# Remainders of up to 32 tokens as a small call on raw weights, in a mixture-of-experts kernel

## The chip, the cores and the metric

One NeuronCore of a Trainium2 chip. The metric is the device time of one execution in microseconds. Engines: PE is TensorE, PEld its weight loads, DVE VectorE, ACT ScalarE, POOL GpSimd, SP the engine that issues most DMAs. "PEldq", "POOLq" and the like are the sequencers' own instructions (loads of registers, branches, waits), which are not counted as busy. [...]

## The reference

Block attention over 4 batches of 768 tokens gives x, 3072 rows of 512. A gate sends each token to one of 8 experts, one after another, and the expert's two layers make the output:

```python
for b in range(B):
    prev_e = -1
    for s in range(S):
        fresh_e = int(np.argmax(logits[b, s]))
        if s == 0 or local_gate[b, s] < 0.5:
            e = fresh_e
        else:
            e = prev_e if prev_e >= 0 else fresh_e
        prev_e = e
        ls = logits[b, s] - logits[b, s].max()
        p = np.exp(ls)
        p /= p.sum() + 1e-09
        h = np.maximum(x[b, s] @ w1[e], 0.0)      # 512 -> 1024
        out[b, s] = p[e] * (h @ w2[e])            # 1024 -> 512
```

Expert weights are 2 x 2 MB of fp32. How many tokens an expert gets depends on the data.

## The kernel before, in words

**Stages.** Attention runs to about 150 us; it writes x to DRAM. The expert calls begin at 133 us and run to the end. Tokens are sorted by expert into 42 slots of 128 rows; slots 0 to 5 (three pairs) are filled early, from the first batches, with the most frequent expert of batch 0 and a second one. `finish` (L782) places the rest: it counts blocks per expert, gives each a first slot, marks in `words` which slots start an expert and which expert comes next, and makes with `rows` (L870) and L961 to L975 the lists `gidx`, `sidx` and `psort` (which token rows a slot gathers, where its results go, and the gate's weight). Its steps are small DVE operations with a few PE products (L884, L949, L971) in between.

**A planner** (`later`, `small`, `flow`, L407 to L471) puts these steps between the matmuls of the running pairs: it keeps a modelled time for PE and for DVE (0.1 us for a small DVE step, 0.9 for a long one, 0.8 for PE) and writes each step where the model says that its input is ready. The order on each engine is then fixed.

**Calls.** `pair` (L1042) handles 256 tokens: for each of 8 column blocks of w1, 4 k-chunks x 3 products of fp32r halves (L1053 to L1055; weights and tokens are split into a high and a low part), then w2 for each half (L1026 to L1028), `store` (L1030: scaling by `psort`, then an indirect DMA to the output at L1039). `single` (L1078) does 128 tokens. Between the matmuls stand the next call's token transposes (`tx`, L1012) and the splitting of the next expert's weights (`split`, L982: ACT makes the high part, DVE or POOL the low one), under `tc.If(new > 0)` (L1234), then the refill of the staging buffer by DMA from SP.

**Order of the calls.** Slots 0 to 15 are eight fixed pairs. From slot 16 on, two slots at a time, a flag decides at run time whether it is a pair or a single; from slot 24 on, a test ends the loop:

```python
nb = reg(2 * SLOTS, mybir.ALL_ENGINES, SLOTS)
with ExitStack() as c:
    for i in range(2 * PAIRS, SLOTS, 2):
        if i >= NT:
            c.enter_context(tc.If(nb > i - EARLY))          # L1295
        two = reg(i + 1, mybir.ALL_ENGINES, 1)
        with tc.If(two > 0) as full:                        # L1298
            ... self.pair(i // 2, *calls(i + 2))
        with full.Else():
            self.single(i, *calls(i + 2))
```

`reg` (L1202) loads a word into a register of each engine named. In the code of every engine the single's instructions stand behind the pair's, and a body that is not run is jumped over; where a skipped body would have raised semaphores, the engine raises them itself, having waited for its own earlier work. A pair has some 310 PE instructions (matmuls and weight loads), a single some 140.

Of the kernel before, what the change touches and what calls it, by code (L numbers as in the profile page):

```python
# [34 lines left out]
PAIRS = 8  # L35
# [29 lines left out]
class Kernel:  # L65
    def __init__(self, ctx, tc, qT, kT, vT, vW, maskc, identc, wgc, w1, w2, c32c, cb16c, out):
# [49 lines left out]
        self.adj = cst.tile([P, 4, E], F32, name="adj")  # L116
        self.zero = cst.tile([P, P], F32, name="zero")
        self.words = cst.tile([1, 2 * SLOTS + 1], I32, name="words")
        self.gidx = cst.tile([P, SLOTS], I32, name="gidx")
        self.sidx = cst.tile([P, SLOTS], I32, name="sidx")  # L120
        self.psort = cst.tile([P, SLOTS], F32, name="psort")
# [3 lines left out]
        for t in (self.zero, self.cnt, self.carx, self.cum):  # L125
            tc.nc.gpsimd.memset(t, 0.0)
# [502 lines left out]
    def second(self):  # L629
# [28 lines left out]
        v.tensor_scalar(out=self.adj[:, 0], in0=self.er, scalar1=-2.0 * 4097, scalar2=6.0 * 4097 + 41344, op0=ALU.mult, op1=ALU.add)  # L658
        yield "DVE"
        v.tensor_scalar(out=self.adj[:, 1], in0=self.er, scalar1=-2.0 * P, scalar2=P - 1.0, op0=ALU.mult, op1=ALU.add)  # L660
        yield "DVE"
        v.tensor_scalar(out=self.adj[:, 3], in0=self.er, scalar1=-2.0 * P, scalar2=2.0 * P - 1.0, op0=ALU.mult, op1=ALU.add)
# [119 lines left out]
    def finish(self):  # L782

        nc, c, cum, wk = self.nc, self.c, self.cum, self.fw
# [9 lines left out]
        v.tensor_scalar(out=npi, in0=nbi, scalar1=8, scalar2=None, op0=ALU.logical_shift_right)  # L794
# [3 lines left out]
        v.tensor_tensor(out=nci, in0=self.cnt[:, B], in1=self.adj[:, 3], op=ALU.add)  # L798
        yield "DVE"
        v.tensor_scalar(out=nci, in0=nci, scalar1=8, scalar2=None, op0=ALU.logical_shift_right)  # L800
# [42 lines left out]
        for b in range(B):  # L843
            yield "DVE"
            v.tensor_tensor(out=t2[:, b], in0=self.oh[:, b], in1=pk.to_broadcast([P, E, NU]), op=ALU.mult)
        pt = wk.tile([P, NT, 1], I32, name="pt")
        yield "DVE"
        with nc.allow_low_precision(reason="whole numbers below 2**24"):
            v.tensor_reduce(out=pt[:, :, 0].rearrange("p (b u) -> p b u", b=B), in_=t2.rearrange("p b e u -> p b u e"),
                            op=ALU.add, axis=AX.X)  # L850
# [40 lines left out]
        start = wk.tile([P, 2, E], F32, name="start")  # L891
# [21 lines left out]
        lv = wk.tile([P, 2, E], F32, name="lv")  # L913
        yield "DVE"
        v.tensor_tensor(out=lv, in0=end, in1=start, op=ALU.is_ge)
# [6 lines left out]
        v.scalar_tensor_tensor(out=en, in0=start, scalar=lane, in1=en, op0=ALU.is_le, op1=ALU.mult)  # L922
        lve = wk.tile([P, 2, E], F32, name="lve")
        yield "DVE"
        v.tensor_tensor(out=lve, in0=lv, in1=c["iota"][:, 0:E].unsqueeze(1).to_broadcast([P, 2, E]), op=ALU.mult)
# [3 lines left out]
        wd = wk.tile([P, 2, 2, E], F32, name="wd")  # L929
# [3 lines left out]
        v.scalar_tensor_tensor(out=wd[:, 1], in0=start, scalar=cend, in1=lve, op0=ALU.is_equal, op1=ALU.mult)  # L933
# [14 lines left out]
        for i in range(2):  # L948
            nc.tensor.matmul(out=m[0:1, SLOTS * i:SLOTS * i + SLOTS], lhsT=w2[:, i:i + 1], rhs=self.ident[:, 0:SLOTS],  # L949
                             start=True, stop=True)  # L950
        yield "DVE"
        v.tensor_copy(out=self.words[:, 2 * SLOTS:], in_=tot)
        yield "DVE"
        v.tensor_copy(out=self.words[:, 0:2 * SLOTS], in_=m[0:1, 0:2 * SLOTS])
# [7 lines left out]
        v.tensor_tensor(out=eq, in0=c["iota"][:, EARLY:SLOTS].unsqueeze(1).to_broadcast([P, NT, n]),  # L962
# [11 lines left out]
        v.tensor_reduce(out=self.psort[:, EARLY:SLOTS], in_=m[:, 0:3 * n].rearrange("p (i s) -> p s i", i=3),  # L974
                        op=ALU.add, axis=AX.X)  # L975
        self.have_p = SLOTS


    def fetch(self, dst, which, c0, c1, e):
# [407 lines left out]
```

## Time and profile before

| | us |
|---|---|
| median of 3 runs | 469.2 (468.76 to 470.35) |
| profiled execution | 469.57, its span 467.8 |
| PE busy in the span | 433.9 (93%) |
| DVE, ACT, POOL busy | 254.4, 213.3, 226.2 |
| last matmul ends | 456.07 |

How to read it: busy times are shares of the span from the first to the last instruction. An engine's idle time is put down to the event that ended it. A group of instructions by line has its count, the total and the mean; a line of windows has the busy time of each engine in one stretch, with the number of instructions in brackets, then the granted clock (PEclk), DMA's busy share and GB/s.

### The profile page before, as it was taken

Reading aid. Unit: us, or ns where it says so; the run is one execution under the profiler, and the core shown is the slowest. Engines: PE = TensorE matmul, PEld = TensorE weight load, DVE = VectorE, ACT = ScalarE, POOL = GpSimd, SP = SyncE. Lnnn points to the kernel's source line nnn. Section 1 sums busy time; section 2 is a strip of 40 time slices with the busy share of each in tenths; the row PEclk is TensorE's granted clock in tenths of the full one; section 3 lists DMA queues with packets and bytes.
Section 4 is the critical chain, followed back from the end, with each engine's and each line's share of the span. In section 5 each row is a group of like instructions: output and inputs, shape, how many; then the busy total and the mean of one; then the engine's idle time right before and its main releaser. Section 6 shows DMA issues by size and latency. Waiting matters only on the chain. (4 is left out here: it accounts for less than half of the span.)

```text
span 467.8 us, 11959 instructions
## 1 busy us (share of the span) xinstructions
PE 433.9 (93%) x4360; PEld 379.9 (81%) x4360; DVE 254.4 (54%) x587; ACT 213.3 (46%) x464; POOL 226.2 (48%) x316
## 2 busy tenths in 40 slices
PE   7799989889699999999999999999999999999990
PEld 6587768767499798888989898988789898978970
DVE  4776797898855788971222222363563227265510
ACT  4888787887645126322212121454582127267300
POOL 2677675687405324912020202193976308488720
PEclk9989999999889999999999999999999999999996
DMA  8999979998230750742020202066579204848940
GB/s 303 378 378 375 378 253 406 377 342 315 89 138 2 262 232 25 275 160 85 12 80 10 82 12 82 6 211 240 205 294 361 85 24 133 320 140 301 320 152 27
DMA packets 23622, 92.04 MB, mean 197 GB/s; under 512 B 2927, under 2 KB 3567, under 8 KB 19440
## 3 DMA queue, kind: packets, MB, share of 16 engines
q1 hardware_dynamic: 18752, 76.11, 43.7%
q0 software_dynamic: 4640, 14.68, 9.9%
q8 instruction: 41, 0.67, 0.6%
q14 instruction: 45, 0.37, 0.2%
q10 hardware_dynamic: 144, 0.20, 0.1%
HBM read 78.40 MB, written 13.11 MB: 196 GB/s over the span
## 5 line engine op out<-in xcount | busy, mean ns | idle before, releaser
L1055 PE MATMUL bs<-xT,l 128*128 128x256 f32 x384 | 109.0, 284 | 1.0 <-DVE l L987 1.0
L1053 PE MATMUL bs<-xT,h 128*128 128x256 f32 x384 | 109.8, 286 | 0.0
L1054 PE MATMUL bs<-xT,h 128*128 128x256 f32 x384 | 108.8, 283 | 0.2 <-DVE xT L1004 0.2
L998 POOL DMA_INDIRECT xg<-x_dram,gidx x32 | 36.8, 1149 | 120.8 <-PE bt L1009 52.3
L1059 ACT ACTIVATE hT<-bs 128x512 fp32r<-128x512 f32 x48 | 28.7, 598 | 121.8 <-PE bs L1055 121.1
L1061 DVE SCALAR_TENSOR_TENSOR hT<-bs,hT 128x512 fp32r<-128x512 f32 x48 | 33.1, 690 | 85.6 <-ACT hT L1059 74.4
L1026 PE MATMUL ba<-h,hT 128*128 128x512 f32 x192 | 77.6, 404 | 0.4
L1028 PE MATMUL ba<-h,hT 128*128 128x512 f32 x192 | 75.0, 391 | 0.0
L1027 PE MATMUL ba<-l,hT 128*128 128x512 f32 x192 | 75.0, 391 | 0.0
L1055 PEld LDWEIGHTS bs<-xT,l 128*128 128x128 f32 x384 | 73.5, 191 | 1.9 <-DVE l L987 1.9
L1054 PEld LDWEIGHTS bs<-xT,h 128*128 128x128 f32 x384 | 73.5, 192 | 1.0 <-DVE xT L1004 0.4
L1053 PEld LDWEIGHTS bs<-xT,h 128*128 128x128 f32 x384 | 73.5, 191 | 0.9 <-issue 0.4
L992 POOL TENSOR_TENSOR l<-stg,h 128x256 fp32r<-128x256 f32 x84 | 73.1, 906 | 2.2 <-ACT h L984 1.6
L984 ACT CAST h<-stg 128x1024 fp32r<-128x1024 f32 x56 | 57.2, 1052 | 11.9 <-PE ba L1028 10.9
L282 ACT ACTIVATE pr<-bs,nm 128x120 f32<-128x120 f32 x192 | 51.9, 371 | 11.5 <-DVE nm L278 9.8
L987 DVE TENSOR_TENSOR l<-stg,h 128x1024 fp32r<-128x1024 f32 x35 | 46.7, 1342 | 16.2 <-ACT h L984 13.1
L1039 POOL DMA_INDIRECT out_dram<-yo,sidx x26 | 28.9, 1113 | 48.8 <-DVE yo L1038 21.3
L1026 PEld LDWEIGHTS ba<-h,hT 128*128 128x128 f32 x192 | 36.1, 188 | 8.1 <-issue 0.5
L1028 PEld LDWEIGHTS ba<-h,hT 128*128 128x128 f32 x192 | 36.0, 188 | 7.9
L1027 PEld LDWEIGHTS ba<-l,hT 128*128 128x128 f32 x192 | 36.2, 188 | 6.2
L243 POOL COPY vw<-vs 24x384 f32<-24x384 f32 x64 | 32.6, 550 | 8.6 <-ACT vs L238 6.1
L278 DVE TENSOR_REDUCE nm<-bs 128x6 f32<-128x720 f32 x32 | 28.8, 901 | 9.2 <-ACT vs L238 4.0
(236 smaller groups left out, 649.3 us busy)
## 6 DMA issues: line engine op xcount, KB each, us to landing
stg<-in_w SPq DMA_DIRECT2D x32, 1024.0 KB, 7.5
vw<-in_vW SPq DMA_DIRECT2D x16, 780.0 KB, 7.1
kp<-in_kT SPq DMA_DIRECT2D x16, 384.0 KB, 6.5
q<-in_qT SPq DMA_DIRECT2D x16, 384.0 KB, 7.5
vt<-in_vT SPq DMA_DIRECT2D x16, 384.0 KB, 8.2
x_dram<-xs SPq DMA_DIRECT2D x8, 768.0 KB, 3.9
wst<-in_w SPq DMA_DIRECT2D x8, 512.0 KB, 5.8
xg<-x_dram,gidx POOLq DMA_INDIRECT x32, 3.5
```

What stands on the lines that cost most here:

```text
L282: nc.scalar.activation(out=pr[:, h, u, :], in_=sp[:, h, u, :], func=AF.Exp, bias=nm[:, h, u:u + 1], scale=1.0)
L984: self.nc.scalar.copy(out=hi, in_=src)
L987: eng.tensor_tensor(out=lo, in0=src, in1=hi.bitcast(F32), op=ALU.subtract)
L992: eng.tensor_tensor(out=lo[:, p], in0=src[:, p], in1=hi[:, p].bitcast(F32), op=ALU.subtract)
L998: self.nc.gpsimd.indirect_dma_start(out=t, out_offset=None, in_=rows, in_offset=bass.IndirectOffsetOnAxis(ap=self.gidx[:, i:i + 1], axis=0))
L1026: nc.tensor.matmul(out=ps, lhsT=ah, rhs=wh, start=first, stop=False)
L1027: nc.tensor.matmul(out=ps, lhsT=ah, rhs=wl, start=False, stop=False)
L1028: nc.tensor.matmul(out=ps, lhsT=al, rhs=wh, start=False, stop=last)
L1053: nc.tensor.matmul(out=ps[:, j], lhsT=wh, rhs=xh, start=(k == 0), stop=False)
L1054: nc.tensor.matmul(out=ps[:, j], lhsT=wh, rhs=xl, start=False, stop=False)
L1055: nc.tensor.matmul(out=ps[:, j], lhsT=wl, rhs=xh, start=False, stop=(k == KT - 1))
L1061: nc.vector.scalar_tensor_tensor(out=l, in0=ps, scalar=0.0, in1=h.bitcast(F32), op0=ALU.max, op1=ALU.subtract)
```

## The change

An expert whose last block holds 1 to 32 tokens (the count plus 127, modulo 128, below 32) no longer gets that block as a slot. It goes to one of up to 8 further columns of the lists (slots 42 to 49), and is computed by `few`: 32 gathered rows, transposed; w1 as fetched, in fp32, without splitting; four column quarters of the product written to four groups of 32 PSUM partitions; then w2 in the same way, four groups of 128 output columns; one scaling and one indirect store of 128 rows of 128 columns. The weights have their own 32 KB per partition, where the lists' temporary tiles were (now in a pool of their own, closed before). The fixed pairs are 7 instead of 8, so the loop with run-time flags starts at slot 14, and its test at slot 22. Small call 0 stands behind the last fixed pair, calls 1 and 2 behind slots 16 and 20, any others behind the loop. Each has a flag and is jumped over if it isn't set; its weights and rows are fetched when the call before it is done.

```diff
-PAIRS = 8
+PAIRS = 7
+FEW = 32
+ALL = SLOTS + E
+CALLS = 11
+FEW_AT = (16, 20)
...
         v.tensor_tensor(out=nbi, in0=self.cnt[:, B], in1=self.adj[:, 1], op=ALU.add)
         yield "DVE"
-        v.tensor_scalar(out=npi, in0=nbi, scalar1=8, scalar2=None, op0=ALU.logical_shift_right)
+        v.tensor_scalar(out=npi, in0=nbi, scalar1=P - 1, scalar2=None, op0=ALU.bitwise_and)
+        lv = wk.tile([P, 3, E], F32, name="lv")
+        few = lv[:, 2]
+        yield "DVE"
+        v.tensor_scalar(out=few, in0=npi, scalar1=float(FEW), scalar2=None, op0=ALU.is_lt)
...
         self.have_words()
-        yield from rows(FIRST, SLOTS)
+
+        yield "DVE"
+        v.scalar_tensor_tensor(out=pk[:, :, 0], in0=self.er, scalar=2.0, in1=nbi, op0=ALU.mult, op1=ALU.add)
...
+        yield from by_expert()
...
+        v.copy_predicated(out=blk, mask=e1, data=pt)
+        yield from rows(FIRST, ALL)
         yield from self.gate_p(B - 1, B)
         yield from self.until(("weights", 0), ("weights", 2))
-        n = SLOTS - EARLY
+        n = ALL - EARLY
...
+        rs = wk.tile([P, 2, E], F32, name="rs")
+        yield "DVE"
+        v.tensor_copy(out=rs[:, 0], in_=self.sidx[:, SLOTS:])
+        yield "DVE"
+        v.tensor_copy(out=rs[:, 1], in_=self.psort[:, SLOTS:])
+        yield "PE"
+        m = self.bank("t")
+        for g in range(4):
+            nc.tensor.matmul(out=m[32 * g:32 * g + 32, 0:2 * E], lhsT=self.ident[:, 0:32], rhs=rs.rearrange("p i e -> p (i e)"),
+                             start=True, stop=True)
...
+    def few_in(self, j, e):
+        nc = self.nc
+        for w in range(2):
+            for c in range(0, KT * DF, 2048):
+                self.fetch(self.few_w[w][:, c:c + 2048], w, c, c + 2048, e)
+        nc.gpsimd.indirect_dma_start(out=self.few_x, out_offset=None, in_=self.x_rows,
+                                     in_offset=bass.IndirectOffsetOnAxis(ap=self.gidx[0:FEW, SLOTS + j:SLOTS + j + 1], axis=0))
+
+    def few(self, j):
+        nc, fw = self.nc, self.fw
+        w1, w2 = self.few_w
+        m = self.bank("t")
+        for k in range(KT):
+            nc.tensor.transpose(out=m[:, FEW * k:FEW * k + FEW], in_=self.few_x[:, P * k:P * k + P], identity=self.ident[0:FEW, 0:FEW])
+        xT = fw.tile([P, KT, FEW], F32, name="few_xT")
+        nc.vector.tensor_copy(out=xT, in_=m[:, 0:KT * FEW].rearrange("p (k t) -> p k t", k=KT))
+        hp = self.bank("s")
+        for k in range(KT):
+            for q in range(4):
+                nc.tensor.matmul(out=hp[32 * q:32 * q + 32, 0:256], lhsT=xT[:, k], rhs=w1[:, k * DF + 256 * q:k * DF + 256 * q + 256],
+                                 start=(k == 0), stop=(k == KT - 1))
+        h = fw.tile([P, 256], F32, name="few_h")
+        nc.scalar.activation(out=h, in_=hp[:, 0:256], func=AF.Relu)
+        m = self.bank("t")
+        for c in range(2):
+            nc.tensor.transpose(out=m[:, P * c:P * c + P], in_=h[:, P * c:P * c + P], identity=self.ident)
+        hT = fw.tile([P, 2, 4, FEW], F32, name="few_hT")
+        nc.vector.tensor_copy(out=hT, in_=m[:, 0:256].rearrange("p (c q t) -> p c q t", c=2, q=4))
+        yp = self.bank("a")
+        for f in range(FT):
+            for d in range(4):
+                nc.tensor.matmul(out=yp[32 * d:32 * d + 32, 0:P], lhsT=hT[:, f % 2, f // 2], rhs=w2[:, f * DM + P * d:f * DM + P * d + P],
+                                 start=(f == 0), stop=(f == FT - 1))
+        y = fw.tile([P, P], F32, name="few_y")
+        nc.vector.tensor_scalar(out=y, in0=yp[:, 0:P], scalar1=self.psort4[:, j:j + 1], scalar2=None, op0=ALU.mult)
+        nc.gpsimd.indirect_dma_start(out=self.out.rearrange("t (q d) -> (t q) d", q=4),
+                                     out_offset=bass.IndirectOffsetOnAxis(ap=self.sidx4[:, j:j + 1], axis=0),
+                                     in_=y, in_offset=None, bounds_check=4 * T_ALL - 1, oob_is_err=False)
...
+            def few(j):
+                with tc.If(reg(SLOTS + j, (ENG.PE, ENG.Activation, ENG.DVE, ENG.Pool), 1) > 0):
+                    self.few(j)
+                few_in(j + 1)
+
+            few_in(0)
             for i in range(EARLY // 2, PAIRS):
                 for _ in self.pair(i, *calls(2 * i + 2)):
                     pass
-            nb = reg(2 * SLOTS, mybir.ALL_ENGINES, SLOTS)
+            few(0)
+            nb = reg(2 * ALL, mybir.ALL_ENGINES, SLOTS)
             with ExitStack() as c:
                 for i in range(2 * PAIRS, SLOTS, 2):
-                    if i >= NT:
+                    if i >= 2 * CALLS:
                         c.enter_context(tc.If(nb > i - EARLY))
...
+                    if i in FEW_AT:
+                        few(1 + FEW_AT.index(i))
+            with ExitStack() as c:
+                for j in range(1 + len(FEW_AT), E):
+                    c.enter_context(tc.If(reg(SLOTS + j, mybir.ALL_ENGINES, 1) > 0))
+                    if j > 1 + len(FEW_AT):
+                        self.few_in(j, reg(ALL + SLOTS + j, (ENG.SP,), E - 1))
+                    self.few(j)
```

## Rows read from the trace of the kernel before

**Rows 1.** The page, parts 1 and 2: busy time of PE and PE's granted clock in 40 slices of the span (tenths).

```profile
PE 433.9 (93%) x4360; PEld 379.9 (81%) x4360; DVE 254.4 (54%) x587; ACT 213.3 (46%) x464; POOL 226.2 (48%) x316
...
PEclk9989999999889999999999999999999999999996
```

**Rows 2.** Groups of PE instructions by line and form: count, then busy us and mean ns of one, then idle us before them.

```profile
...
L1055 PE MATMUL bs<-xT,l 128*128 128x256 f32 x384 | 109.0, 284 | 1.0 <-DVE l L987 1.0
...
L1026 PE MATMUL ba<-h,hT 128*128 128x512 f32 x192 | 77.6, 404 | 0.4
...
L1026 PE MATMUL bs<-h,xT 128*128 128x512 f32 x16 | 6.5, 406 | 0.5 <-PE ba L1028 0.5
```

**Rows 3.** Windows: stretches from the first matmul of a call to that of the next. Columns: us, busy us (instructions) of PE, PEld, DVE, ACT and POOL, granted clock, DMA share, GB/s. In order: the two pairs beside which the placing runs, the pair behind them, a plain fixed pair, the last fixed pair (a single follows), that single, the pair behind it, and the stretch behind the last matmul.

```profile
164.75:190.54 25.79, 25.79 (x217) 23.02 (x216) 22.59 (x93) 11.77 (x15) 9.87 (x9) 1.00 0.28 109
190.54:217.38 26.84, 25.65 (x202) 23.18 (x200) 16.95 (x32) 6.02 (x10) 11.75 (x12) 1.00 0.59 207
217.38:240.74 23.36, 23.36 (x153) 21.31 (x152) 4.90 (x7) 4.25 (x7) 3.99 (x4) 1.00 0.15 46
...
287.47:310.84 23.37, 23.37 (x154) 21.32 (x152) 10.62 (x13) 10.58 (x13) 9.06 (x8) 1.00 0.15 41
310.84:334.80 23.96, 23.30 (x150) 20.69 (x148) 12.00 (x13) 11.49 (x14) 16.34 (x17) 1.00 0.63 230
334.80:347.73 12.93, 12.93 (x64) 10.70 (x65) 6.09 (x8) 7.91 (x12) 10.43 (x14) 1.00 0.86 340
347.73:372.08 24.35, 23.84 (x153) 21.41 (x152) 9.90 (x12) 7.37 (x10) 12.79 (x14) 1.00 0.69 239
...
456.07:467.79 11.72, 0.00 (x0) 0.00 (x0) 0.75 (x1) 0.00 (x0) 1.00 (x1) 0.64 0.09 27
```

**Rows 4.** Timeline of PE: start, us, instruction. The gate's fp32 products into three groups of 32 partitions (two records for each product), and four transposes in a single.

```profile
141.79 1.07 PE L495 MATMUL bt<-hs,wg 128*32 128x128 f32 x24
...
422.83 0.60 PE L1009 MATMUL bt<-ident,hs 128*128 128x128 f32 x4
```

**Rows 5.** Groups by line and form on DVE and ACT: copies out of PSUM, relu, and operations of the placing.

```profile
L967 DVE TENSOR_TENSOR bp<-eqp,p 128x864 bf16<-128x864 f32 x3 | 3.1, 1052 | 0.0
...
L880 DVE TENSOR_TENSOR bt<-eq,c 128x768 bf16<-128x768 f32 x2 | 2.9, 1441 | 0.0
...
L962 DVE TENSOR_TENSOR eqp<-c,blk 128x864 f32<-128x864 f32 x1 | 1.1, 1052 | 0.0
...
L875 DVE TENSOR_TENSOR eq<-c,blk 128x768 f32<-128x768 f32 x1 | 0.9, 936 | 0.0
...
L845 DVE TENSOR_TENSOR t<-oh,pk 128x48 f32<-128x48 bf16 x4 | 0.6, 203 | 0.0
...
L504 DVE COPY l_all<-bt 128x27 f32<-128x27 f32 x2 | 0.3, 175 | 0.0
...
L1089 ACT ACTIVATE hs<-bs 128x512 f32<-128x512 f32 x4 | 2.4, 598 | 5.6 <-PE bs L1028 5.6
...
L499 ACT COPY l<-bt 96x128 f32<-96x128 f32 x2 | 0.5, 262 | 0.4 <-PE bt L495 0.4
```

**Rows 6.** Timeline of all engines where a pair ends whose successor, a single, has a new expert: start, us, instruction, and idle us before it.

```profile
...
333.90 0.39 PE L1028 MATMUL ba<-h,hT 128*128 128x512 f32 x1
334.10 1.23 DVE L987 TENSOR_TENSOR l<-stg,h 128x1024 fp32r<-128x1024 f32 x1 [1.44 <-ACT h L984]
...
334.80 0.47 PE L1026 MATMUL bs<-h,xT 128*128 128x512 f32 x1 [0.51 <-PE ba L1028]
...
335.24 0.74 DVE L1038 TENSOR_SCALAR yo<-ba,psort 128x512 f32<-128x512 f32 x1
```

**Rows 7.** Lines asked for one by one, PE's sequencer alone: count, ns of one (least, median, most), first and last start. Word loads at 330.1; jumps from the test to the single's code, twice; the jump out of the loop; the jump from the pair's end past the single's code; the signal of a skipped body.

```profile
L1203 PEldq TENSOR_LOAD <-words x2: 300/311/322, 330.1 to 330.5; - x2
...
L1298 PEldq COMPARE_BRANCH  x1: 3732/3732/3732, 330.9 to 330.9; - x1
...
L1298 PEldq COMPARE_BRANCH  x1: 2619/2619/2619, 415.6 to 415.6; - x1
...
L1292 PEldq COMPARE_BRANCH  x1: 3887/3887/3887, 452.1 to 452.1; - x1
...
L1298 PEldq COMPARE_BRANCH  x1: 304/304/304, 368.0 to 368.0; - x1
...
L1244 PEldq EVENT_SEMAPHORE  x1: 51/51/51, 327.1 to 327.1; - x1
```

**Rows 8.** Waits of PE in the two pairs beside which the placing runs: us in total, times, longest.

```profile
PE bt L884 <- DVE bt L880: 0.7, 1, 0.7
PE bt L971 <- DVE bp L967: 0.5, 1, 0.5
```

**Rows 9.** Lines asked for one by one, POOL's sequencer at the end: count, ns, start.

```profile
L1292 POOLq INC_SWDGE_SEM  x1: 1328/1328/1328, 460.6 to 460.6; - x1
...
L1382 POOLq DRAIN  x3: 46/107/4813, 462.2 to 467.5; - x3
```

**Rows 10.** Windows: stretches of about 3.4 us around two falls of the granted clock.

```profile
121.54:124.96 3.42, 0.92 (x24) 0.81 (x24) 2.65 (x7) 2.66 (x7) 3.36 (x5) 1.00 0.25 61
124.96:128.37 3.41, 1.93 (x18) 1.24 (x19) 2.35 (x9) 0.48 (x1) 1.12 (x3) 0.50 0.77 241
...
459.46:462.80 3.34, 0.00 (x0) 0.00 (x0) 0.00 (x0) 0.00 (x0) 0.00 (x0) 0.50 0.04 11
```

More of the change, by code (lines that the diff above doesn't have):

```diff
@@ L124, in __init__ @@
         nc.vector.memset(self.wz, 0.0)
-        for t in (self.zero, self.cnt, self.carx, self.cum):
+        for t in (self.zero, self.cnt, self.carx, self.cum, self.before):
             tc.nc.gpsimd.memset(t, 0.0)
@@ L842, in finish, with by_expert @@
         t2 = wk.tile([P, B, E, NU], F32, name="t2")
-        for b in range(B):
-            yield "DVE"
[L845 to L850, printed above, removed]
+        pt = wk.tile([P, NT, 1], I32, name="pt")
+        def by_expert():
+            for b in range(B):
+                yield "DVE"
+                v.tensor_tensor(out=t2[:, b], in0=self.oh[:, b], in1=pk.to_broadcast([P, E, NU]), op=ALU.mult)
+            yield "DVE"
+            with nc.allow_low_precision(reason="whole numbers below 2**24"):
+                v.tensor_reduce(out=pt[:, :, 0].rearrange("p (b u) -> p b u", b=B), in_=t2.rearrange("p b e u -> p b u e"),
+                                op=ALU.add, axis=AX.X)
+        yield from by_expert()
         blk = wk.tile([P, NT, 1], F32, name="blk")
@@ L912, in finish @@
         v.scalar_tensor_tensor(out=end[:, 1], in0=nci, scalar=2.0, in1=end[:, 1], op0=ALU.mult, op1=ALU.add)
-        lv = wk.tile([P, 2, E], F32, name="lv")
         yield "DVE"
-        v.tensor_tensor(out=lv, in0=end, in1=start, op=ALU.is_ge)
+        v.tensor_tensor_scan(out=self.before[:, 1:E + 1], data0=few, data1=self.zero[:, 0:E], initial=0.0, op0=ALU.add, op1=ALU.add)
+        yield "DVE"
+        v.tensor_scalar(out=start[:, 2], in0=self.before[:, 0:E], scalar1=SLOTS + 1.0, scalar2=None, op0=ALU.add)
+        yield "DVE"
+        v.tensor_tensor(out=lv[:, 0:2], in0=end, in1=start[:, 0:2], op=ALU.is_ge)
         yield "DVE"
@@ L1144, in have_rows @@
             st["rows"] = s1
-            while st["next"] < min(s1, st["free"]):
+            while st["next"] < min(s1, SLOTS, st["free"]):
                 self.gather(st["next"])
@@ L1221, in start @@
                 if s not in r:
-                    r[s] = reg(s, (ENG.SP, ENG.Activation, ENG.DVE, ENG.Pool), 1), reg(SLOTS + s, (ENG.SP,), E - 1)
+                    r[s] = reg(s, (ENG.SP, ENG.Activation, ENG.DVE, ENG.Pool), 1), reg(ALL + s, (ENG.SP,), E - 1)
                 return r[s]
@@ L1264, in run @@
             sp = ctx.enter_context(tc.tile_pool(name="stage", bufs=1))
+            places = ctx.enter_context(ExitStack())
+            self.gw = places.enter_context(tc.tile_pool(name="g_wk", bufs=1, side="right"))
             st["spent"] = []
@@ L1287, in run, with few_in @@
             assert "words" in st and self.have_p == SLOTS
+            places.close()
+            fp = ctx.enter_context(tc.tile_pool(name="few", bufs=1, side="right"))
+            self.few_w = [fp.tile([P, KT * DF], F32, name=f"few_w{w}") for w in range(2)]
+            self.few_x = fp.tile([FEW, DM], F32, name="few_x")
+            def few_in(j):
+                is_, e = reg(SLOTS + j, (ENG.SP, ENG.Pool), 1), reg(ALL + SLOTS + j, (ENG.SP,), E - 1)
+                with tc.If(is_ > 0):
+                    self.few_in(j, e)
+            def few(j):
[3 more added lines that the diff above has]
+            few_in(0)
             for i in range(EARLY // 2, PAIRS):
@@ L1323, in consts @@
          "s8": 8.0 * (lane + P * np.arange(NU, dtype=np.float32)) + 8.0,
-         "iota": one * np.arange(SLOTS, dtype=np.float32),
+         "iota": one * np.arange(ALL, dtype=np.float32),
          "iota128": one * np.arange(P, dtype=np.float32),
@@ L1328, in consts @@
          "odd": lane % 2,
-         "sum4": (np.arange(P)[:, None] % 32 == np.arange(G9)[None, :]).astype(np.float32),
+         "quarter": np.floor(lane / 32),
          "sel127": sel127}
```

71 lines of the change are left out of this document (48 added, 23 removed).

## The prediction

> **What bounds the kernel now.** I began with the busy shares: PE works 93% of the span, at full clock in nearly every slice [rows 1]. No other engine comes near, so time is what PE has to do plus the moments when it must wait. The groups by line then give the calls: L1055 runs 32 times in a pair and L1026 16 times, so 384 and 192 are twelve pairs; a single has 8 L1026 on its first product, so 16 are two singles [rows 2]. That is 26 blocks, and the reference's routing of its inputs says the same: experts 0, 2, 3, 4, 6 get 1, 768, 1400, 768 and 135 tokens, that is 1 + 6 + 11 + 6 + 2 blocks. The stretches from call to call give the prices [rows 3]: a plain pair 23.37 us, all of it PE busy; a single 12.93; a pair behind a single 24.35 (it waits for its weights); and behind the last matmul 11.72 us in which PE does nothing.
>
> **What goes.** Expert 0 has a remainder of 1 and expert 6 of 7; both are within 32. 24 full blocks stay: eleven pairs and two singles. Expert 3's 120 tokens still take a single, expert 6's pair becomes a single, expert 0's single becomes a small call. So exactly one pair leaves PE's path and two small calls come. The pair at 310.84 cost 23.96 with the jump behind it, of which 0.08 moves to its neighbour: **-23.9 us**. Two weight switches fewer are worth nothing: in both kernels two pairs stand behind a single and wait about 1 us, and the other splits lie beside PE work.
>
> **The arithmetic of a small call.** The nearest row for fp32 products in column groups is L495: twelve 128x32 products of 128 columns are 24 records in 1.07 us [rows 4], three groups at once. Taking off one record's 0.30 leaves 7 steps of 0.11. With four groups, the first product is 4 k-chunks x 2 records x 256 columns, 8 steps of 0.22 = 1.74 us; the second 8 x 2 steps of 0.109, again 1.74. Between them lie hand-overs in which PE has nothing else, since the call stands alone: a DVE copy of 128 columns, 0.29 (between 0.175 for 27 columns and 0.74 for 512), the relu on ACT of 256 columns, 0.37 (between 0.26 for 128 and 0.60 for 512) [rows 5, 6], two transposes, 0.38 (four take 0.60 [rows 4]), a copy of 256 columns, 0.45, and some 0.5 for fill and signals.
>
> Call 0 stands behind the pair that splits the weights of slot 14, so I read the like place at 334 [rows 6]. PE's array is free at 334.13, but DVE starts a split at 334.10 and the output scaling at 335.24, until 335.98. The copy of the transposed tokens queues behind both and is done 2.2 us after the array is free. 2.2 + 1.74 + 0.37 + 0.38 + 0.45 + 1.74 + 0.5 is **7.4 us**. Call 1 stands behind a pair without a split; only the scaling is ahead, 0.9 less: 6.5. The weights cost nothing: 4 MB each, loaded in a stretch in which DMA is 15% busy (217.38) or during the 36 us between the calls. If that cover is gone, 4 MB at the 340 GB/s of a busy stretch [rows 3] are 12 us.
>
> **The jumps.** This is where I expect the gain to go. PE's sequencer needs 3.73 and 2.62 us for the jump into the single's code, past the pair's, and 3.89 past the rest of the loop; past the single's code only 0.30 [rows 7]. Today it starts at 330.1 on its word loads and PE's last matmul starts at 333.90: it is about 17 matmuls (3.8 us) ahead, and of 3.73 only 0.51 shows [rows 6, 7]. Behind a small call the same 17 records are 17/4 x 0.109 = 0.46 us. Then come a short jump (0.2), two word loads (0.8 from 330.1 to 330.9), the jump (3.18, the mean) and 0.1 of signals: 4.3 - 0.46 = **3.9 us** idle before slot 14's single; 3.3 and 4.4 by the two rows. Call 0 is 11.3 in all. Behind call 1 comes a pair, no jump: one word load and a test, 0.3 net, **6.8**. [...] The 17 of the rows are what I use.
>
> Call 2 has no tokens and is jumped over, but not for nothing. Where a body is skipped now, PE itself waits at the skip's signal (L1244, 327.1 [rows 7]): it is drained and the lead is gone. Right behind it stands the jump into slot 22's single: 0.25 + one load 0.4 + tests 0.15 + 3.18 + 0.15, **4.1 us**, where today there is no gap. Bounds 3.5 and 5.3 (the jump over the small call's own 210 or so PE instructions lies between the 0.30 and the 3.73 row, and starts under cover).
>
> **The placing.** In the two pairs over which it lies, PE takes 25.79 and 26.84 us instead of 23.36 [rows 3], and waits for DVE 0.7 before L884 and 0.5 before L971 [rows 8]: DVE's chain already comes last there. The wide index grows from 32 to 40 columns, the weights from 36 to 44: seven wide DVE operations, 8.0 us in all, by a quarter, 1.9 us, and some 14 small ones of 0.2 each (L845) [rows 5], 2.9 us, of which the planner foresees about 2. PE's own part is 0.55. Bounds 0.6 and 4; taken **+2.5**, nearer to the upper end, as the two waits show no slack.
>
> **The tail.** Behind the last store, POOL steps its counters (1.33 us in one instruction) and drains for 4.81 [rows 9]. The second nest of skipped small calls, with indirect stores in it, adds a word load on every engine, tests, and a like stepping: 0.4 + 0.6 + 1.3, **+2.3**. Below: 0, if the drain's end is set by the store's landing. Above: 5, if POOL or DVE must make a second far jump.
>
> **The clock.** [...] Half clock for 3.41 us loses 1.7 of work at most, less where the gap itself lies in it: **+2.3** for both. Bounds 0 and 6.8 (two stretches each).
>
> **Sum.** -23.9 + 11.3 + 6.8 + 4.1 + 2.5 + 2.3 + 2.3 = +5.4. The profiled execution took 469.57 (span 467.8), so 475.0; the median of the runs, 469.2, is 0.4 below it: **474.6 us**. About 0.3%, 1.4 us, is what a measurement of this kernel tells from no change.
>
> **Rivals.** *Faster: the jumps cost little.* If the far jumps find their code at hand, or PE's sequencer keeps its lead, call 0 is 8.1, the skip 0.9, and the clock has no gap to fall in: -23.9 + 8.1 + 6.8 + 0.9 + 2.5 + 2.3 = -3.3, **465.9 us**. The point that decides: jumps and clock together are 8.7 of my sum, and the change breaks even when 5.4 of them are missing. For it: only half a microsecond of any far jump shows today. Against: all three far PE jumps took 2.6 to 3.9 us in the sequencer. [...] Chance 0.20.
>
> *Slower still: the four groups do not run side by side.* Then each product takes four times 1.74, a small call 10.4 more, the whole 20.8: **495 us**. Against it stand L495's 24 records in 1.07 us, which one after the other would take 2.6. Chance 0.04.
>
> *The change doesn't do what it says.* If no flag is found set, the small calls are skips and PE does eleven pairs and two singles plus three drains: about 461 us. The counts above speak against it. Chance 0.02.
>
> **The numbers.** My forecast, with its own range of 469 to 481 (each term between its bounds, not all at one end), has 0.74. Most of its lower edge is within 0.3%; so faster 0.20, same 0.10, slower 0.70. The range takes in the first rival: 464.5 to 481.5.
>
> **What would show it.** Right: eleven pairs, two singles, two small calls of 6 to 8 us up to their last matmul; a PE gap of 3 to 4.5 us before each of the two singles, ended by PE's own sequencer; the granted clock at 0.50 near 320 and 430; PE waits before L884 and L971 of 1 to 3 us; 12 to 16 us from the last matmul to the end. Wrong: gaps below 1 us at those places (first rival), a small call over 12 us, or a small call that waits for a DMA.

## The result, and the profile after

The changed kernel takes **474.17 us** (median of 4 runs, 473.9 to 476.87); the kernel before, on the same chip, 469.77. The ratio is 1.0107, 95% interval 1.0062 to 1.0151: slower by more than the 0.3% that a measurement here can tell, and 0.4 us from the 474.6 forecast. The profiled execution took 474.1, its span 472.3, that is 4.5 more than before. The sum was right, but two of its terms were far off in opposite directions; the stretches show where.

Windows of the changed kernel, columns as in [rows 3]. In order: the second of the pairs beside which the placing runs (the first, from 165.03, took 25.66); small call 0; slot 14's single; small call 1; the pair behind which call 2 is skipped; the stretch behind the last matmul; and the two halves of the stretch at the lower clock from 200.75.

```profile
190.69:224.70 34.01, 28.39 (x211) 25.59 (x209) 23.54 (x50) 6.00 (x11) 10.82 (x13) 0.90 0.43 163
...
318.32:326.56 8.24, 4.76 (x104) 3.18 (x103) 2.74 (x5) 1.43 (x2) 7.51 (x10) 1.00 1.01 404
326.56:341.95 15.39, 12.98 (x64) 10.70 (x65) 4.75 (x6) 7.15 (x11) 5.69 (x7) 1.00 0.93 363
...
365.77:372.30 6.53, 4.76 (x103) 3.17 (x103) 1.39 (x3) 0.38 (x1) 1.01 (x1) 1.00 0.12 44
...
395.76:420.52 24.76, 23.31 (x149) 20.68 (x148) 11.70 (x13) 11.16 (x13) 10.44 (x9) 1.00 0.19 64
...
457.98:472.27 14.29, 0.00 (x1) 0.00 (x0) 0.75 (x1) 0.00 (x0) 1.01 (x1) 0.58 0.09 26
...
200.75:204.17 3.42, 1.12 (x18) 1.12 (x19) 2.85 (x4) 0.00 (x0) 0.00 (x0) 0.50 0.99 399
204.17:207.57 3.40, 3.40 (x24) 3.40 (x23) 2.12 (x13) 0.24 (x1) 0.00 (x0) 0.50 0.46 192
```

Waits of PE in the changed kernel from 164 us on: us in total, times, longest. L899 is the index product (before: L884), L1080 lies in slot 14's single, L1397 is the small call's flag.

```profile
PE bt L899 <- DVE bt L895: 5.6, 1, 5.6
PE bs L1080 <- issue: 2.4, 1, 2.4
PE bs L1189 <- DVE few_xT L1185: 2.3, 2, 1.6
PE bs L1079 <- ACTq L1397: 1.3, 1, 1.3
```

The sequencers alone, as in [rows 7, 9]: count, ns (least, median, most), first and last start. PE's two L1413 branches around slot 14's single (the first is the jump to its code), the two around slot 22's (the second is that jump), then POOL's stepping for the loop and for the nest.

```profile
L1413 PEldq COMPARE_BRANCH  x2: 71/269/467, 325.9 to 339.6; - x2
...
L1413 PEldq COMPARE_BRANCH  x2: 179/298/417, 415.0 to 419.9; - x2
...
L1407 POOLq INC_SWDGE_SEM  x1: 1337/1337/1337, 462.8 to 462.8; - x1
...
L1421 POOLq INC_SWDGE_SEM  x1: 1308/1308/1308, 465.3 to 465.3; - x1
```

What the reader is to see, as a second sum:

| step | forecast | measured | read from |
|---|---|---|---|
| pair removed | -23.9 | -23.96 | [rows 3] |
| call 0, its arithmetic | 7.4 | 7.37 | 8.24 less a gap of 0.87 before the single |
| the jump behind call 0 | 3.9 | 3.33 | 0.87, and the single's 15.39 - 12.93 |
| call 1 | 6.8 | 6.53 | its window |
| call 2's skip and jump | 4.1 | 1.47 | 24.76 against 23.29 for that pair before |
| placing | 2.5 | 4.78 | waits 5.62 - 1.19, and PE's own 0.35 |
| clock | 2.3 | 2.26 | half of 1.12 + 3.40 busy at 0.50 |
| tail | 2.3 | 2.57 | 14.29 - 11.72 |
| other pairs, and the start | 0 | +0.13 | the rest |
| sum | +5.4 | +4.48 | |

The jumps and the clock were to cost 10.3 and cost 4.8 where they were expected. The first rival broke even when 5.4 of them were missing, and 5.5 were. What kept the change slower is the placing: 2.5 forecast, 4.8 measured, with a further 2.3 for the clock, which fell there and at neither of the two places named.

### The profile page after: what moved, and what is told of

Same layout as the page of the kernel before. It is cut to its first block, busy times and chain, and to the rows that moved or that the text cites. A ratio compares the mean times of both kernels' runs of the same rounds, so it can differ in the third digit from the quotient of the medians.

```text
span 472.3 us, 12027 instructions
## 1 busy us (share of the span) xinstructions
PE 424.7 (90%) x4420; PEld 367.6 (78%) x4420; DVE 244.9 (52%) x596; ACT 194.2 (41%) x444; POOL 203.0 (43%) x293
## 3 DMA queue, kind: packets, MB, share of 16 engines
q0 software_dynamic: 4448, 14.29, 8.9%
## 5 line engine op out<-in xcount | busy, mean ns | idle before, releaser
L1106 PE MATMUL bs<-xT,h 128*128 128x256 f32 x352 | 101.7, 289 | 0.1
L1108 PE MATMUL bs<-xT,l 128*128 128x256 f32 x352 | 100.4, 285 | 0.4 <-POOL l L1045 0.2
L1107 PE MATMUL bs<-xT,h 128*128 128x256 f32 x352 | 100.3, 285 | 0.2 <-DVE xT L1057 0.2
L1079 PE MATMUL ba<-h,hT 128*128 128x512 f32 x176 | 71.2, 404 | 0.4
L1106 PEld LDWEIGHTS bs<-xT,h 128*128 128x128 f32 x352 | 68.0, 193 | 1.2 <-issue 0.7
L1081 PE MATMUL ba<-h,hT 128*128 128x512 f32 x176 | 68.9, 391 | 0.0
L1080 PE MATMUL ba<-l,hT 128*128 128x512 f32 x176 | 68.9, 391 | 0.0
L1108 PEld LDWEIGHTS bs<-xT,l 128*128 128x128 f32 x352 | 68.0, 193 | 1.1 <-DVE l L1040 0.6
L1107 PEld LDWEIGHTS bs<-xT,h 128*128 128x128 f32 x352 | 68.1, 193 | 0.8 <-DVE xT L1057 0.6
L1045 POOL TENSOR_TENSOR l<-stg,h 128x256 fp32r<-128x256 f32 x60 | 51.7, 895 | 7.8 <-ACT h L1037 7.2
L1037 ACT CAST h<-stg 128x1024 fp32r<-128x1024 f32 x40 | 40.5, 1051 | 6.9 <-PE ba L1081 5.9
L1040 DVE TENSOR_TENSOR l<-stg,h 128x1024 fp32r<-128x1024 f32 x25 | 34.0, 1374 | 10.5 <-ACT h L1037 7.5
L1079 PEld LDWEIGHTS ba<-h,hT 128*128 128x128 f32 x176 | 33.1, 188 | 7.5 <-issue 0.6
L1081 PEld LDWEIGHTS ba<-h,hT 128*128 128x128 f32 x176 | 33.0, 188 | 7.2
L1080 PEld LDWEIGHTS ba<-l,hT 128*128 128x128 f32 x176 | 33.2, 189 | 5.7
```

The lines of the kernel that those rows point to most:

```text
L1037: self.nc.scalar.copy(out=hi, in_=src)
L1040: eng.tensor_tensor(out=lo, in0=src, in1=hi.bitcast(F32), op=ALU.subtract)
L1045: eng.tensor_tensor(out=lo[:, p], in0=src[:, p], in1=hi[:, p].bitcast(F32), op=ALU.subtract)
L1079: nc.tensor.matmul(out=ps, lhsT=ah, rhs=wh, start=first, stop=False)
L1080: nc.tensor.matmul(out=ps, lhsT=ah, rhs=wl, start=False, stop=False)
L1081: nc.tensor.matmul(out=ps, lhsT=al, rhs=wh, start=False, stop=last)
```

## The experiments

**1. What makes the placing late.** Timeline of DVE and POOL in the changed kernel, just behind the words: start, us, instruction.

```profile
190.93 6.60 POOL L1045 TENSOR_TENSOR l<-stg,h 128x256 fp32r<-128x256 f32 x8
...
192.71 0.66 DVE L980 SCALAR_TENSOR_TENSOR pk<-pk,start 128x8 f32<-128x8 f32 x1
...
194.81 2.79 DVE L859 TENSOR_TENSOR t<-oh,pk 128x48 f32<-128x48 bf16 x4
...
198.16 0.18 DVE L987 TENSOR_SCALAR e<-pt 128x24 int32<-128x24 int32 x1
```

Seven of the new small DVE steps take 0.66 to 0.70 each (the first 0.47) while POOL makes the low parts of the second expert's weights, and 0.18 once POOL is done. They stand ahead of the wide index operations, for which PE waits. Three theories: it is these steps; it is the lists that grew from 32 to 40 columns; it is POOL beside them.

*before_steps*: the kernel before, with the new steps alone, on scratch tiles, and lists as wide as before. The cut holds twelve more: three on pk2, four products, a sum and four on 24 columns.

```diff
         self.have_words()
+        pk2 = wk.tile([P, E, 1], F32, name="pk2")
+        yield "DVE"
+        v.scalar_tensor_tensor(out=pk2[:, :, 0], in0=self.er, scalar=2.0, in1=nbi, op0=ALU.mult, op1=ALU.add)
...
         yield from rows(FIRST, SLOTS)
```

> The kernel before, with the 13 small DVE steps added at the same place behind the words, on scratch tiles; lists, calls and code else unchanged. Theory (the steps cost, not the small calls nor the wider lists): PE's wait before the index product grows from 0.7 us to 4 or 5, the granted clock falls as in the changed kernel, and the time is 4 to 7 us above the kernel before, 474 to 477. Rival (the eight further columns of the lists make the wait): the wait stays under 2 and the time within 2 us.

Measured: 475.43 (473.28 to 476.32), ratio 1.0103, 1.0057 to 1.0148. Timeline, then PE's waits:

```profile
192.03 5.66 POOL L1020 TENSOR_TENSOR l<-stg,h 128x256 fp32r<-128x256 f32 x8
...
192.14 0.71 DVE L962 SCALAR_TENSOR_TENSOR pk<-pk,lv 128x8 f32<-128x8 f32 x1
...
193.58 2.76 DVE L971 TENSOR_TENSOR t<-oh,pk 128x48 f32<-128x48 bf16 x4
```

```profile
PE bt L884 <- DVE bt L880: 3.6, 1, 3.6
```

The 0.7 of [rows 8] became 3.6 (4 or 5 were expected), and the granted clock fell right behind it, for 3.41 us from 202.05. The steps alone bring most of the wait, with no small call in the kernel and the lists as they were. The other 2.0 of the changed kernel's 5.6 may belong to the wider lists; no run has the lists alone.

*no_pool_split*: the changed kernel, without POOL's low parts in that one split: its chunks are skipped, and the second expert's weights are then incomplete.

```diff
-                    split(w, chunks)
+                    split(w, chunks, None)
```

> The changed kernel without POOL's share of the second expert's weight split (three of its eight low parts stay stale; the output is wrong by that). Theory (the small DVE steps are slow because POOL works beside them): the steps behind the words take 0.15 to 0.25 us each instead of 0.47 to 0.70, the chain from the words to the index product is 4 us shorter, and PE's wait falls from 5.6 to 2 us or less. Rival (the steps are that slow by themselves, each waiting for the one before): the durations and the wait stay.

Measured: 473.25 (one time), span 471.4. Timeline, then PE's waits (lines moved by 0 to 2):

```profile
191.97 0.17 DVE L980 SCALAR_TENSOR_TENSOR pk<-pk,start 128x8 f32<-128x8 f32 x1
...
192.58 0.62 DVE L859 TENSOR_TENSOR t<-oh,pk 128x48 f32<-128x48 bf16 x4
```

```profile
PE bs L1081 <- issue: 5.0, 1, 5.0
...
PE bt L899 <- DVE bt L895: 1.0, 1, 1.0
```

The same steps took 0.17 and 0.155 each, the wait fell from 5.6 to 1.0, and the clock stayed up there; the pair took 27.39 (190.85 to 218.24) instead of 34.01. So it is POOL that makes the steps slow. But 5.0 now stands before slot 14's single, where 0.87 and 2.41 stood, and ate the gain: the second theme, below.

*plan_long*: the changed kernel, with the planner told that eight of these steps (four on pk, the four products) are long, 0.9 instead of 0.1, and with one more pair to place them beside.

```diff
-        yield "DVE"
+        yield "LONG"
...
-            rest = chain(first, *(self.pair(i, *calls(2 * i + 2)) for i in range(1, EARLY // 2)))
+            rest = chain(first, *(self.pair(i, *calls(2 * i + 2)) for i in range(1, EARLY // 2 + 1)))
```

> The changed kernel with one edit: the planner is told 0.9 us instead of 0.1 for eight of the small DVE steps behind the words (and may lay the placing over one pair more), so PE's index product is written some 6 us later among the matmuls of the third pair. Theory (the placing's steps are slow on DVE and the planner doesn't know it): PE's wait of 5.6 us before the index product falls under 1.5, the granted clock doesn't fall there, and the time drops by 5 to 8 us, to 466 to 469. Rival (PE has nothing else to do: the pair's own results queue on DVE behind the same steps): the wait moves to the pair's matmuls, and the time drops by less than 2.

Measured: 469.97 (467.77 to 472.79), ratio 0.9994, 0.996 to 1.0029. The same stretch, and PE's waits:

```profile
190.69:224.70 34.01, 34.01 (x269) 31.27 (x268) 23.86 (x50) 8.15 (x14) 12.47 (x14) 1.00 0.48 176
```

```profile
PE bs L1080 <- issue: 2.1, 1, 2.1
PE bs L1079 <- issue: 1.8, 1, 1.8
```

PE is busy for all of the 34.01 (28.39 in the changed kernel), at full clock: most of the steps are as slow as they were, but PE has matmuls while they run. 4.2 us came back, less than the 5 to 8 expected, and the change is level with the kernel before. In this run call 0 takes 9.2 instead of 7.4, as the clock now falls within it, and the stalls at slot 14's single are 3.9 instead of 3.3.

*fill_wait*: 24 idle matmuls into the wait, so that PE does not stand still.

```diff
             m = self.bank("t")
+            for t in range(24 if n > 8 else 0):
+                nc.tensor.matmul(out=m[:, 0:512], lhsT=self.wz, rhs=self.A[:, 0:4, :].rearrange("p t l -> p (t l)"), start=True, stop=True)
             for t in range(NT):
```

> The changed kernel with 24 idle matmuls of 512 bf16 columns (5.2 us, zeros as weights, into the bank that the index product then overwrites) written just before the index product, where PE stood idle. They wait for nothing. Theory (the fall of the clock is a cost of its own, 2.3 us, set off by the idle time): the granted clock stays at 1.00 there and the time drops by 1.5 to 3 us, to 471 to 473. Rival (the clock's fall lies beside the wait and costs nothing, or has another cause): the time stays within 0.7 us or grows.

Measured: 480.75 (479.0 to 484.0), ratio 1.0235, 1.0175 to 1.0294. The time went the other way, though the place behaved as the theory has it: the wait left is 0.4, the granted clock in 190.69 to 224.70 is 1.00, and the pair takes 31.96 (192.21 to 224.17) instead of 34.01. The 2.05 saved are near the 2.26 taken above for the fall of the clock. The largest loss is at slot 14's single again, with the clock at 0.50 from 328.89 for 6.83 us; 1.7 more is a later start of the calls in this execution:

```profile
PE bs L1081 <- issue: 6.4, 1, 6.4
...
PE bt L901 <- DVE bt L895: 0.4, 1, 0.4
```

**2. What the jump behind call 0 costs.** Its cost had now been 3.3, 3.9, 5.2 and 6.4 in four kernels whose call 0 is the same. PE's sequencer shows two kinds of far jump: in the changed kernel 0.467, with a stall of 2.41 in the middle of the single (a page of 16,384 bytes on the instruction queue starts at 329.81 and takes 0.97); in fill_wait 5.957 at the jump itself. The 2.41 stands behind the single's 13th matmul, and 2.05 in plan_long at the same place. The profile names no cause for such stalls ("issue"). That PE waits for code is my reading of the instruction queue: in each of the nine stalls of over 1.5 us in these runs, a page lands 1.3 to 2.0 us before PE goes on (1.38 in the changed kernel, 330.78 against 332.16). The theory became: PE has no lead behind a short call, so whatever code is not there yet shows in full, at the jump or a page later.

*few_shift*: the small calls stand where a pair follows, behind slots 16 and 18, and slot 14's single stands behind a full pair again; call 2 is left to the nest.

```diff
-FEW_AT = (16, 20)
+FEW_AT = (16, 18)
...
-            few(0)
...
-                        few(1 + FEW_AT.index(i))
+                        few(FEW_AT.index(i))
...
-                for j in range(1 + len(FEW_AT), E):
+                for j in range(len(FEW_AT), E):
```

> The changed kernel with its two small calls moved: call 0 behind slot 16, call 1 behind slot 18, each with a pair behind it, and call 2 left to the nest behind the loop; the jump to slot 14's single again stands behind a full pair. Theory (what the jumps cost is not the jump itself but that PE's sequencer has lost its lead behind a short call, and then the code of the single must be fetched): the gap before slot 14's single and the 2.41 in it go, and so does the 1.30 at the skipped call 2; 3 to 5 us less than the changed kernel, 469 to 471.5. Rival (the stall belongs to the single's code, however PE comes to it): a stall of 2 us or more stays in or before slot 14's single, and the time stays within 1.5 us of 474.

Measured: 470.91 (468.9 to 472.82), ratio 1.0014, 0.9992 to 1.0037. PE's waits from 164 us on (what is left out are the two hand-overs within the small calls, 1.1 and 1.0), and the window of the tail:

```profile
PE bt L899 <- DVE bt L895: 5.6, 1, 5.6
PE bs L1189 <- DVE few_xT L1185: 1.8, 2, 1.1
PE bs L1108 <- DVE l L1040: 1.6, 2, 1.1
...
```

```profile
451.98:468.00 16.02, 0.00 (x0) 0.00 (x0) 0.75 (x1) 0.00 (x0) 1.01 (x1) 0.57 0.07 23
```

No wait for "issue" is left, and none at a skip, though the jump to slot 14's single takes 3.333 in PE's sequencer. PE ends at 451.98, 6.0 earlier; 1.9 of it is an earlier start of the calls in this execution (131.35 against 133.22). The tail gave 1.7 back (16.02 against 14.29). The stall is not the single code's own; it is the missing lead.

*few_in_late*: call 1's 4 MB fetched behind slot 14's single, so that they do not move beside the code's pages.

```diff
                     self.few(j)
-                few_in(j + 1)
+                if j:
+                    few_in(j + 1)
...
+                    if i == 14:
+                        few_in(1)
                     if i in FEW_AT:
```

> The changed kernel with the 4 MB of weights and the rows of call 1 fetched only behind slot 14's single instead of right behind call 0. The stall of 2.41 us in that single came while those transfers held the DMA queues. If the code's fetch waits behind the weights, the stalls from call 0's end to the next pair (0.87 and 2.41) shrink below 1.5 us in sum. If the price is the fetch of a page that is not at hand, they stay at 2.5 to 4.5 in sum, and call 1 may wait for its weights (4 MB at 340 GB/s are 12 us, under a pair's 23 of cover).

Measured: 481.17 (one time). PE's longest wait in 315 to 345, the jump, and a window from the small call to the end of that wait (columns as in [rows 3]):

```profile
PE bs L1079 <- issue: 4.1, 1, 4.1
```

```profile
L1414 PEldq COMPARE_BRANCH  x1: 3587/3587/3587, 329.3 to 329.3; - x1
```

```profile
317.60:333.10 15.50, 8.13 (x111) 4.77 (x110) 3.68 (x6) 2.81 (x4) 9.57 (x11) 0.86 0.92 316
```

The stall grew from 3.3 to 4.1, so call 1's weights are not what the code waits for. Other transfers are not ruled out: DMA was still 0.92 busy, with the refill of the staging buffer among others, and the page took 2.63 on its queue (from 328.92) instead of 0.97. This edit touches no instruction of PE, yet the jump went from 0.467 to 3.587: how much shows does not depend on the layout of PE's code alone. The total is a single time with the clock at 0.50 twice around call 0 and the single (from 321.92 and from 332.16); its other microseconds I do not explain further.

*single_first*: the single's code ahead of the pair's, so that slot 14's single stands directly behind call 0.

```diff
-                    with tc.If(two > 0) as full:
-                        for _ in self.pair(i // 2, *calls(i + 2)):
-                            pass
+                    with tc.If(two < 1) as lone:
+                        self.single(i, *calls(i + 2))
                     st.update(kept)
-                    with full.Else():
-                        self.single(i, *calls(i + 2))
+                    with lone.Else():
+                        for _ in self.pair(i // 2, *calls(i + 2)):
+                            pass
```

> The changed kernel with the two bodies of each run-time slot pair in the other order: the single's code stands first, the pair's behind it, so that slot 14's single follows call 0's code directly. Theory (behind a short call PE's sequencer has no lead, and code that does not stand next has to be fetched first, whether it stalls at the jump or a page later): the stalls at slot 14 (0.87 and 2.41) come to less than 1.5 in sum; a pair now stands past 140 PE instructions, so the pair behind call 1 may get 0.5 to 3 in front of it; net 1 to 3 us less, 471.5 to 473.5. Rival (a page is fetched on demand every so many instructions and shows wherever the lead is gone, jump or not): the stalls stay at 2.5 to 4.5 in sum, and the time at 473.5 to 476.

Measured: 479.09 (476.36 to 480.86), ratio 1.0155, 1.0116 to 1.0195. PE's waits in 315 to 350, and the jump from the single's end past the pair's code. The profile lists it under the single's last statement, L1330; in PE's sequencer slot 16's word load follows it:

```profile
PE bs L1106 <- issue: 4.7, 1, 4.7
...
PE bs L1079 <- PE ba L1201: 0.6, 1, 0.6
```

```profile
L1330 PEldq COMPARE_BRANCH  x1: 3041/3041/3041, 337.4 to 337.4; - x1
```

Half a hit. At slot 14 only 0.6 is left, as the theory has it. But the time rose: a stall of 4.7 stands in the pair behind the single, three matmuls in (a page starts at 344.14, the stall ends at 346.59), with the clock down from 343.55. The sequencer was 2.9 us ahead at the single's end: the jump starts at 337.37, the last matmul ends at 340.32. The far jump, which now stands there, takes 3.04 and uses this lead up, so the page missing next shows in full. The clock fell within call 0 as well (for 3.41 us from 319.66). Rearranging the code moved this cost here; what hid a far jump (few_shift's 3.333) was a full pair ahead of it.

**3. The tail.** *no_nest*: without the nest of small calls behind the loop (calls 3 to 7 are left out; none has tokens here).

```diff
-            with ExitStack() as c:
-                for j in range(1 + len(FEW_AT), E):
...
-                    self.few(j)
```

> The changed kernel without the nest of skipped small calls behind the loop. Theory (the nest's word load, tests and counter stepping lie on the path to the end): from PE's last matmul to the end 11.7 to 12.2 us instead of 14.3, 471.5 to 472.5 us in all. Rival (the drain's end is set by the last store's landing, and the nest runs beside it): 14 us stay behind the last matmul, 474 in all. In either case the code is shorter, and the stalls at the jumps may come out otherwise; the stretch behind the last matmul decides.

Measured: 475.36 (473.69 to 477.15), ratio 1.0124, 1.0088 to 1.0159. The stretch behind the last matmul, and the jump to slot 14's single:

```profile
459.81:471.86 12.05, 0.00 (x1) 0.00 (x0) 0.75 (x1) 0.00 (x0) 1.01 (x1) 0.63 0.09 29
```

```profile
L1413 PEldq COMPARE_BRANCH  x1: 3050/3050/3050, 325.6 to 325.6; - x1
```

The tail fell by 2.24, as the theory has it. The total did not fall: the jump went from 0.467 to 3.050, and the clock fell behind it.

**4. Do the four groups run side by side?** *groups_serial*: the same 48 products of a small call, one group after the other.

```diff
-        for k in range(KT):
-            for q in range(4):
+        for q in range(4):
+            for k in range(KT):
...
-        for f in range(FT):
-            for d in range(4):
+        for d in range(4):
+            for f in range(FT):
```

> The changed kernel with the loops of the small call's two products turned round: all k-chunks of one column quarter one after the other, then the next quarter, so that neighbouring matmuls write the same 32 PSUM partitions; the same 48 matmuls, the same sums. If the four groups run side by side only when they alternate, each product takes three times 1.9 us more and a small call some 11 more, the whole about 22 more: 495 to 498. If the four groups never ran side by side, or do so in either order, the small calls stay at 8.2 and 6.5 us and the whole at 474, but for the stalls at the jump.

Measured: 485.51 (one time). PE's groups by form over both small calls, of the changed kernel and of groups_serial:

```profile
L1201 PE MATMUL ba<-few_w,few_hT 128*32 128x128 f32 x128 | 3.9, 274 | 1.0 <-DVE few_hT L1197 1.0
L1189 PE MATMUL bs<-few_w,few_xT 128*32 128x256 f32 x64 | 3.9, 382 | 2.3 <-DVE few_xT L1185 2.3
```

```profile
L1201 PE MATMUL ba<-few_w,few_hT 128*32 128x128 f32 x120 | 11.0, 274 | 1.0 <-DVE few_hT L1197 1.0
L1189 PE MATMUL bs<-few_w,few_xT 128*32 128x256 f32 x64 | 9.2, 382 | 2.9 <-DVE few_xT L1185 2.9
```

Each matmul takes as long as before (382 and 274 ns), but the union of them grows 2.4 and 2.8 times, not 4 times: call 1 took 11.59 instead of 6.53. Side by side is real, and it is worth 5.1 us a call here, half of what was expected: a group by itself still overlaps its own successive matmuls (64 of 382 ns in 9.2 us). The run also bears on the second theme: call 0's second product is 4.0 us longer here (5.95 against 1.95), the gap before slot 14's single is gone, and 1.8 is left, again behind its 13th matmul.

**5. Both repairs together.** *both*: plan_long's and few_shift's edits.

> The changed kernel with the planner told that the new small DVE steps are long and the placing's rest reaching over one more pair, and the small calls behind slots 16 and 18. If the two costs are separate, their gains add: 4.2 for the placing (measured alone) and 3 to 5 for the calls' places: 465 to 467 us, 0.6 to 1% below the kernel before. If the placing's gain and the calls' places pay for the same thing (PE's lead and the clock), it is 468 to 470, level with the kernel before.

Measured: **464.24** (462.6 to 464.94), ratio 0.9863, 0.9836 to 0.9891. PE's waits, PE's branches around slot 14, and the stretch behind the last matmul:

```profile
PE bs L1189 <- DVE few_xT L1185: 1.8, 2, 1.1
PE bs L1108 <- DVE l L1040: 1.6, 2, 1.1
...
PE bs L1079 <- PE ba L1081: 0.5, 1, 0.5
```

```profile
L1412 PEldq COMPARE_BRANCH  x3: 71/290/3673, 307.2 to 344.2; - x3
```

```profile
446.53:463.10 16.57, 0.01 (x1) 0.00 (x0) 0.75 (x1) 0.00 (x0) 1.01 (x1) 0.63 0.07 23
```

The two gains do not pay for the same thing: against the changed kernel's 474.17, the medians save 4.2 (plan_long), 3.3 (few_shift) and 9.9 (both). The 2.4 beyond the sum are about what plan_long by itself lost again behind the placing, 1.9 in call 0 and 0.5 at slot 14. The far jump to slot 14's single still takes 3.673, and shows only the 0.5 of the last row of waits, as in [rows 6]: the lead of a full pair hides it. The granted clock stayed at 1.00 from 133.4 to 450.9, behind the last matmul. The small calls are worth up to 1.4% here, once their two side costs are hidden. Some of it may be the planner's: the kernel before waits 1.2 us for the placing [rows 8], this one not at all, and plan_long's extra pair was not tried on the kernel before. What is left to gain stands behind the last matmul: 16.57 us, 4.9 more than before, of which no_nest puts some 2.2 down to the nest; in both POOL's last store waits for the landing of the store before it (5.79 us idle).

## Why the prediction was right, and where it was not

**Right in mechanism and size.** The pair (-23.9, -23.96), call 0's arithmetic (7.4, 7.37), call 1 (6.8, 6.53) and the tail (2.3, 2.57) came as worked out. Within call 0 two parts were off the other way: each product took 1.95 instead of 1.74, and it was 2.0 until the tokens were copied, not 2.2. The 0.9 between the calls came too: PE waits 1.6 for the copied tokens where a split is ahead, 0.7 where none is. That the groups run side by side was taken from L495, and experiment 4 shows it; the price of the rival in which they do not (10.4 a call) was twice the measured 5.1, since one group overlaps its own matmuls.

**"The jumps": the sum behind call 0 was right, the step not.** It had PE's sequencer spend 3.18 at the jump, uncovered (its terms add up to 3.8, not 3.9). The jump took 0.467, and 2.41 came 13 matmuls later. By the prediction's own signs the gap of 0.87 before the single, below 1, spoke for the first rival; the cost stood inside the single, where no sign had been set. Where call 0 is as long as here the price was 3.3 to 6.4, so the forecast 3.9 (3.3 to 4.4) was near the low end, and the jump rows of before could not show the upper one. That the lead is what counts, and that a small call takes it away, is shown by few_shift (3.333, hidden) and both (3.673, hidden).

**"Call 2 is skipped": mis-sized**, 4.1 against 1.47. PE is drained at the skip as foreseen, but the far jump behind it took 0.417, not 3.18, and ran beside the wait for ACT's signal, which ended last (1.3). The step took a far jump's time for a property of the jump. The far jumps in these runs are of two kinds: 0.34 (groups_serial) to 0.47 (the changed kernel), or 2.6 [rows 7] to 6.0 (fill_wait); what sets them apart was not shown. Nor does the cost come at jumps alone: the 2.4 in the single stands 3.3 us behind the jump, in straight code. The 4.7 in single_first stands close behind two taken jumps (3.041 and 0.226) and may belong to either. Near branches took 65 (L1413 in the changed kernel) to 304 ns [rows 7].

**"The placing": mis-sized, and with its clock the largest miss**, 2.5 against 4.78, above its upper bound of 4, and with the fall of the clock 7.0. (Its parts, 1.9 + 2.9 - 2 + 0.55, add up to 3.35; 2.5 was taken.) The step that failed is the price of a small DVE step, 0.2 from L845 [rows 5], a row of a stretch without POOL. Beside POOL's split it is 0.66 to 0.70; no_pool_split gives the 0.2 back. This stood in the trace of before, in rows that the prediction did not use: DVE's index steps and POOL, timeline of the kernel before, in the second of the two pairs.

```profile
190.24 8.06 POOL L992 TENSOR_TENSOR l<-stg,h 128x256 fp32r<-128x256 f32 x8
...
196.35 0.60 DVE L775 TENSOR_SCALAR gidx<-g 128x32 int32<-128x32 f32 x1
196.87 0.78 DVE L778 TENSOR_SCALAR tl<-tl 128x32 f32<-128x32 f32 x1
```

Eight steps ran beside POOL; at 0.5 more each they are 4, so 2.5 + 4 is more than the 4.78. In before_steps POOL's eight take 5.66, 0.71 each, and the DVE steps take 0.66 to 0.71, about one to each of POOL's; why they lengthen beside POOL the profile does not show. The planner's 0.1 for such a step is what plan_long repairs.

**"The clock": size right, place wrong.** The term counts two falls, in the gaps before the two singles, each with the 3.41 us at 0.50 of the second stretch of [rows 10]. The clock was low once, from 200.75 to 207.57; it fell within the 5.62 that PE waited (197.43 to 203.05), and not at 320 or 430, where the gaps were 0.87 and 1.3. That one fall there cost what two were to cost elsewhere is chance. before_steps (3.6 of wait, fall), plan_long (none, no fall there) and fill_wait (0.4, no fall there) tie it to the wait; no_nest and fill_wait show that it does fall behind call 0 when the stall there is 3.5 or 6.4. In plan_long it fell for 3.41 us (from 313.49) within call 0 itself, where PE waits 1.6 for the copied tokens, ahead of the jump at 321.5; so there it fell without a jump.

So that the forecast time came within 0.4 us is luck: -5.5 on the jumps and their clock and +4.5 on the placing and its clock nearly cancel. The first rival's mechanism (jumps that cost little) came half true; its 465.9 is, by chance too, near what the repaired kernel takes.

What stays open: what decides whether a far jump takes 0.47 or 3.59 with the same code of PE, and so the 3.3 to 6.4 behind call 0. Whether the pages queue behind other transfers was not tested apart from call 1's weights.

## What to carry to other kernels

A call that is cheap in arithmetic (7.4 us here) is dear where it stands if its engine's sequencer needs the matmuls ahead as cover (3.3 to 6.4 us more here): put short calls between long ones, and not in front of a far jump. Read the price of a small DVE step in the very stretch where it will run, with what POOL does beside it (0.17 or 0.66 to 0.70 here), and not from a mean. And when a forecast comes true, take its terms apart all the same: here the two worst cancelled, and repairing both turned 1% slower into 1.4% faster.

## What the runs showed of the hardware

- A DVE operation on 8 columns takes 0.14 to 0.17 alone (no_pool_split) and mostly 0.66 to 0.71 beside POOL's TENSOR_TENSOR (the changed kernel, before_steps); a one-input TENSOR_SCALAR (L984) takes 0.67 there and 0.17 alone.
- PE stalled in straight code too, behind the same 13th matmul in three kernels in which a small call had just run: 2.41 us in the changed kernel, 2.05 in plan_long, 1.8 in groups_serial; a page itself takes 1.0 on the DMA queue there, and lands 1.3 to 1.4 before PE goes on.
- The same far jump, to slot 14's single, takes 0.34 (groups_serial) to 0.47 (the changed kernel) or 3.0 (no_nest) to 6.0 (fill_wait) in PE's sequencer; behind a full pair, 3.3 of it is hidden in few_shift, and all but 0.5 of 3.7 in both.
- Records of fp32 matmuls with 128x32 weights and 256 columns follow each other at 0.144 us into one group of 32 PSUM partitions (groups_serial, 9.2 over 64), at 0.061 into four groups in turn (the changed kernel, 3.9 over 64).
